# Local and global attention units issued in pairs, with the gate's part moved and the scores further ahead

## The chip, the cores and the metric

The kernel runs on one core of a Trainium2 chip. The core has a matrix engine (TensorE; PE in the profile, with its weight loads shown apart as PEld), a vector engine (VectorE, DVE), a scalar engine for activations (ScalarE, ACT), a general engine (GpSimd, POOL) and a queue engine that issues DMAs (SyncE, SP). Each takes its instructions in the order of the program. The metric is the device time of one execution in microseconds (us), lower is better. A program's time is the median of several runs, and one further execution is recorded by the hardware profiler.

## The reference, cut to what matters

There are 8 batches of 8 heads. Each head has 512 local tokens, 32 global tokens and a width of 64. A local token looks at local tokens within 32 places and at all global tokens; a global token looks at everything.

```python
k_all = np.concatenate([k_g, k_l], axis=2)
s_g = scale * np.matmul(q_g, k_all.transpose(0, 1, 3, 2))
out_g = np.matmul(sm(s_g), v_all)
s_ll = scale * np.matmul(q_l, k_l.transpose(0, 1, 3, 2))
s_ll = np.where(np.abs(pos[:, None] - pos[None, :]) <= 32, s_ll, -1000000000.0)
s_lg = scale * np.matmul(q_l, k_g.transpose(0, 1, 3, 2))
out_l = np.matmul(sm(np.concatenate([s_lg, s_ll], -1)), np.concatenate([v_g, v_l], axis=2))
x = np.concatenate([out_g, out_l], axis=2)
...
logits = x @ w_gate
...
h = np.maximum(x[mask] @ w1[e], 0.0)
out[mask] = h @ w2[e]
```

`sm` is a softmax. The attention rows (4352 rows of 512) go to a mixture of 8 experts: all logits are sorted, each row goes to its best expert that still has room (544 rows each), and each expert is two matrix products with a ReLU between.

## The kernel before

The program has two parts, one after the other: `attention`, which also makes the gate's logits `L`, and `experts`, which starts with a search for the routing over all logits. The change touches `attention` alone.

**Units.** Attention is cut into 80 units, ten for each batch. A `Local` unit takes 256 query rows of one pair of heads (eight per batch); a `Glob` unit takes the global rows of four heads (two per batch). In a batch the order is four Locals, a Glob, four Locals, a Glob; in the last batch two Locals, both Globs, six Locals. Every unit has four steps:

- `a`: the scores, matmuls into PSUM tiles named `S` (L134; of a Glob L195). A Local takes one bank, a Glob two (`sa`, `sb`).
- `e`: on VectorE the mask is added and the row maximum taken (L141), then scaled (L143); on ScalarE four exponentials (L145) write `p`. Of a Glob, the maxima are L201 to L203 and the exponentials L210 to L216, into `pg`, read straight from the two `S` banks.
- `c`: `p` is transposed on TensorE into banks `T` (L150; of a Glob L224, two banks) and copied to SBUF as `pt` or `pgt` by `evac`.
- `d`: the products with the values, into banks `O` (L162; of a Glob L234), then on VectorE the division by the row sums (L165, L166, L170; of a Glob L237 to L241), and DMAs of `xs` or `xg` to DRAM.

PSUM has three banks `S`, three `T` and two `O`. `evac` (L248) shares copies out in the order in which the program makes them: of every five, three go to ScalarE (L251) and two to VectorE (L253).

**The gate's part.** The logits of a batch are made by six small steps (`gate_units`): four times `gate_x` (four transposes of `xs`, L259, and a copy to `xt`), `gate_m` (matmuls with the gate's weights into an `O` bank, L265, and a copy to `ltc`), and `gate_l` (four transposes of `ltc`, L274, and a sum into `L` on VectorE, L275). They stand in a table `extra`, keyed by the number of the iteration: for most batches at 1, 3, 5, 7, 9 and 10 units after the batch's end plus ten; for the batch before the last at six successive units. The global rows of four batches are read back (`load_gx`) and get six steps of the same kind with one block of rows.

**The loop.** It runs over units `i`, with the scores two ahead. TensorE gets, in one iteration, S of unit i+2, T of unit i, O of unit i-1, then the gate's step if there is one. In the program's order `e` of unit i+2 stands between the transposes and the outputs:

```python
units[i + LA].a()
units[i].c()
units[i + LA].e()
units[i - 1].d()
for f in extra.get(i, []): f()
```

Ahead of `a`, SP issues loads of `q`, `qk` and `vw` for the pair of heads four further on; POOL spreads `q` into `qz` (L86). In the last iterations the first steps of the routing (`first`, VectorE, seen as L405) are put in six at a time.

Of the kernel before, what the change touches and what calls it, by code (L numbers as in the profile page):

```python
# [8 lines left out]
F32 = mybir.dt.float32  # L9
# [9 lines left out]
B, H, SL, SG, D = 8, 8, 512, 32, 64  # L19
S = SL + SG  # L20
DM = H * D
# [4 lines left out]
NB = SL // 128  # L26
NW = SL // 32
# [8 lines left out]
def ap_of(t, offset, dims):  # L36
    return bass.AP(tensor=t.tensor, offset=t.offset + offset, ap=dims)
# [27 lines left out]
def attention(ctx, tc, A, consts, xd, ident, L, nbatch, rt=None):  # L65
    nc = tc.nc
    ac = ctx.enter_context(tc.tile_pool(name="ac", bufs=1))
    ld = ctx.enter_context(tc.tile_pool(name="ld", bufs=3))
    wk = ctx.enter_context(tc.tile_pool(name="wk", bufs=3))
# [3 lines left out]
    qk, vw, xs = {}, {}, {}  # L73

    def load_qk(b, p):
        t = ld.tile([128, KW], F32, name="qk", bufs=5)
        q = ld.tile([128, QW], F32, name="q", bufs=3)
        z = qz[(b * NP + p) % NZ]
        nc.sync.dma_start(q, A["qk"][b, p, :, :QW])
        nc.sync.dma_start(t, A["qk"][b, p, :, QW:])  # L80
        qk[b, p] = t

        def spread(eng):
            for h in range(2):
                r = slice(64 * h, 64 * h + 64)
                eng.tensor_copy(z[r, :, h, :], q[r].rearrange("p (j i) -> p j i", i=32))  # L86
        return spread

    def load_v(b, p):
        t = ld.tile([128, 2, NW, D + 1], F32, name="vw", bufs=6)  # L90
        nc.sync.dma_start(t.rearrange("p h w d -> p (h w d)"), A["vw"][b, p])
        vw[b, p] = t

    qz = [ac.tile([128, QW // 32, 2, 32], F32, name=f"qz{i}") for i in range(NZ)]
    pg = [ac.tile([128, 6, 128], F32, name=f"pg{i}") for i in range(2)]
    mask = ac.tile([128, 2 * NB, 128], F32, name="mask")
    wg = ac.tile([128, 4, 32], F32, name="wg")
    P = [(b, p) for b in range(nbatch) for p in range(NP)]
# [6 lines left out]
    for i in range(NZ):  # L105
        nc.gpsimd.memset(qz[i][64:128, :, 0, :], 0.0)
        nc.gpsimd.memset(qz[i][0:64, :, 1, :], 0.0)
    for i in range(2):
        nc.gpsimd.memset(pg[i], 0.0)
    load_qk(0, 0)(nc.vector)  # L110
    nc.sync.dma_start(mask.rearrange("p a b -> p (a b)"), A["mask"])
# [1 line left out]
    spread1 = load_qk(0, 1)  # L113
# [5 lines left out]
    class Local:  # L119
# [3 lines left out]
        def a(s):  # L123
            b, q = s.b, s.q
            z = qz[(b * NP + q) % NZ]
            kw = qk[b, q]
            st = ps.tile([128, NB, 128], F32, name="S", bufs=3)
            s.p = wk.tile([128, NB, 128], F32, name="p", bufs=4)
            s.nm = wk.tile([128, NB], F32, name="nm", bufs=4)
            for c in range(NB):  # L130
                for r in range(2):
                    j = 8 * s.u + 2 * c + r
                    k0 = 32 * ((3 * j + 1) // 2)
                    nc.tensor.matmul(st[64 * r:64 * r + 64, c, :], z[:, j].rearrange("p h i -> p (h i)"),  # L134
                                     kw[:, k0:k0 + 128], start=True, stop=True)
            s.st = st

        def e(s):
            st, nm = s.st, s.nm
            for c in range(NB):  # L140
                nc.vector.tensor_tensor_reduce(s.p[:, c, :], st[:, c, :], mask[:, 4 * s.u + c, :], 1.0, -BIG,  # L141
                                               ALU.add, ALU.max, nm[:, c:c + 1])
            nc.vector.tensor_scalar(nm, nm, -SCALE, None, op0=ALU.mult)  # L143
            for c in range(NB):
                nc.scalar.activation(s.p[:, c, :], s.p[:, c, :], AF.Exp, bias=nm[:, c:c + 1], scale=SCALE)  # L145
# [29 lines left out]
    class Glob:  # L175
# [20 lines left out]

        def e(s):
            b, g = s.b, s.g
            m = wk.tile([128, 8], F32, name="gm", bufs=2)
            s.m = m  # L200
            nc.vector.tensor_reduce(m[:, 0:1], s.sa, axis=AX.X, op=ALU.max)  # L201
            nc.vector.tensor_reduce(m[:, 1:2], s.sb, axis=AX.X, op=ALU.max)
            nc.vector.tensor_scalar(m[:, 2:3], m[:, 0:1], m[:, 1:2], -SCALE, op0=ALU.max, op1=ALU.mult)  # L203
            pgt = pg[(b * 2 + g) % 2]
            s.p = pgt
            f = pgt.rearrange("p a b -> p (a b)")
            d0 = f[:, 0:64]
            d1 = f[:, 512:576]
            pd = list(d0.ap[0])
            nc.scalar.activation(ap_of(d0, 0, [pd, [256, 2], [96, 3], [1, 64]]),  # L210
                                 s.sa[:, 0:384].rearrange("p (a b c) -> p a b c", a=2, c=64), AF.Exp,
                                 bias=m[:, 2:3], scale=SCALE, accum_out=m[:, 3:4])
            nc.scalar.activation(ap_of(d1, 0, [pd, [192, 2], [1, 64]]),
                                 s.sa[:, 384:512].rearrange("p (b c) -> p b c", c=64), AF.Exp,
                                 bias=m[:, 2:3], scale=SCALE, accum_out=m[:, 4:5])
            nc.scalar.activation(f[:, 672:704], s.sb, AF.Exp,  # L216
                                 bias=m[:, 2:3], scale=SCALE, accum_out=m[:, 5:6])
# [30 lines left out]
    def evac(dst, src):  # L248
        nev[0] += 1
        if nev[0] % 5 < 3:  # L250
            nc.scalar.activation(dst, src, AF.Copy)  # L251
        else:
            nc.vector.tensor_copy(dst, src)  # L253

    def gate_x(src, xt, c, spare):
        t = ps.tile([128, NB, 128], F32, name="S" if spare else "T", bufs=3)
        n = src.shape[1]
        for k in range(n):
            nc.tensor.transpose(t[:, k, :], src[:, k, c * 128:(c + 1) * 128], ident)  # L259
        evac(xt[:, c, :n * 128], t[:, :n].rearrange("p a b -> p (a b)"))  # L260

    def gate_m(xt, n):
        lt = ps.tile([128, 512], F32, name="O", bufs=2)
        for c in range(4):
            nc.tensor.matmul(lt[32 * c:32 * c + 32, :n * 128], wg[:, c, :], xt[:, c, :n * 128],  # L265
                             start=True, stop=True)
        ltc = wk.tile([128, 512], F32, name="ltc", bufs=2)
        evac(ltc[:, :n * 128], lt[:, :n * 128])
        return ltc

# [7 lines left out]
    def gate_units(b, src, J, n):  # L278
        xt = []

        def go(c):
            if c == 0:
                xt.append(wk.tile([128, 4, 128 * n], F32, name=f"xt{n}", bufs=2))
            if c < 4:
                gate_x(src(), xt[0], c, b == nbatch - 1)
            elif c == 4:
                xt.append(gate_m(xt[0], n))
            else:
                gate_l(xt[1], J, n)
        return [lambda c=c: go(c) for c in range(6)]  # L290
# [1 line left out]
    gsrc = {}  # L292

    def load_gx(i):
        t = wk.tile([128, 1, DM], F32, name="gx", bufs=2)
        for k in range(4):
            nc.sync.dma_start(t[32 * k:32 * k + 32, 0, :], xd[(4 * i + k) * S:(4 * i + k) * S + SG, :])
        gsrc[i] = t

    units = []  # L300
    for b in range(nbatch):
        loc = [Local(b, h) for h in range(H)]
        gl = [Glob(b, g) for g in range(2)]
        if b < nbatch - 1:
            us = loc[:4] + [gl[0]] + loc[4:] + [gl[1]]
        else:
            us = loc[:2] + gl + loc[2:]
        units += us
    extra = {}
    GS = (0, 2, 4, 6, 8, 9)  # L310
    for b in range(nbatch):
        last = b == nbatch - 1
        s0 = 10 * (b + 1) + 1
        gl = gate_units(b, lambda b=b: gsrc[b // 4], 32 + b // 4, 1) if b % 4 == 3 or last else []
# [13 lines left out]
    nl = [3]  # L328

    def pairidx(u):  # L330
        if isinstance(u, Local):
            return u.b * NP + u.q
        return u.b * NP + 2 * u.g + 1

    nu = len(units)
    first = rt.setup(slice(0, 28)) if rt else None
    LA = 2
    for i in range(-LA, nu + 3):
        if rt and i == 2:
            rt.load()  # L340
        if rt and i == 12:
            rt.prepare()
        if i + LA < nu:
            while nl[0] < len(P) and nl[0] <= pairidx(units[i + LA]) + 4:
                load_qk(*P[nl[0]])(nc.gpsimd)
                load_v(*P[nl[0] - 1])
                nl[0] += 1
                if nl[0] == len(P):
                    load_v(*P[-1])
            units[i + LA].a()  # L350
        if 0 <= i < nu:
            units[i].c()
        if i + LA < nu:
            units[i + LA].e()
            if i + LA == 0:
                spread1(nc.vector)
        if 1 <= i <= nu:
            units[i - 1].d()
        for f in extra.get(i, []):
            f()  # L360
        if rt and i >= nu - 3:
            for _ in range(6):
                next(first, None)


# [638 lines left out]
```

## Time and profile before

| | us |
|---|---|
| timed runs: 752.65, 748.70, 749.91; median | 749.91 |
| the profiled execution's own time | 756.55 |
| its span, first to last instruction | 754.5 |
| attention, up to the first search matmul (L473) | 0 to 236.9 |

The profile's page gives busy times per engine, the span in 40 slices, and groups of instructions by line. The windows view gives the busy times of the engines in a stretch of time. The timeline lists instructions in order of time, with those of one kind merged: start, time from the first start to the last end, engine, line, operation, what it writes and reads, the tile's shape, its count, and in brackets the idle time of the engine before it and what ended that. Matmuls are pipelined, so the rows of two successive groups overlap; what a group takes of TensorE's time is the distance between the starts.

### The profile page before, as it was taken

The page shows a single profiled execution, that of the slowest core. Times are in us where ns is not written, and L with a number is a line of the kernel's source. Part 1 is how long each engine was busy: PE and PEld are TensorE (multiplying, and loading weights), DVE is VectorE, ACT ScalarE, POOL GpSimd, SP SyncE. Part 2 cuts the span into 40 slices and gives each one's busy share as a digit, 9 for nine tenths or more (in the row PEclk, how much of TensorE's full clock was granted, in tenths as well). Part 3 has the DMA queues.
Part 4 walks back from the last instruction along what each step waited for, and adds up shares of the span by engine and source line. Part 5 has one row for each costly group of instructions (what it writes and reads, how often), then busy time and mean ns, then how long its engine had stood idle before and what let it go on. Part 6 is the DMA issues. An engine that isn't in the chain of part 4 may idle for free. (4 is left out here: it accounts for less than half of the span.)

```text
span 754.5 us, 21122 instructions
## 1 busy us (share of the span) xinstructions
PE 697.2 (92%) x8636; PEld 560.2 (74%) x8636; DVE 504.8 (67%) x1848; ACT 313.8 (42%) x849; POOL 159.7 (21%) x190
## 2 busy tenths in 40 slices
PE   7989999999995189999999999999999999899993
PEld 6767777777673179768779878877877878888972
DVE  5887878877777778767767777766776774441300
ACT  3656665665651034234143244234333333443310
POOL 5222112221100130241241241141132043312011
PEclk9999999999998569999999999999999999999997
DMA  9997879969701160360161161261072065231000
GB/s 359 405 364 286 323 280 332 338 244 333 289 22 58 45 238 1 111 204 29 70 234 40 62 240 43 71 212 62 8 260 78 1 254 186 75 126 46 1 33 28
DMA packets 32416, 120.51 MB, mean 160 GB/s; under 512 B 6720, under 2 KB 6976, under 8 KB 24128
## 3 DMA queue, kind: packets, MB, share of 16 engines
q1 hardware_dynamic: 22080, 67.78, 24.1%
q0 software_dynamic: 10240, 51.39, 19.4%
q8 instruction: 68, 1.11, 0.6%
q14 instruction: 28, 0.23, 0.1%
HBM read 101.32 MB, written 17.83 MB: 158 GB/s over the span
## 5 line engine op out<-in xcount | busy, mean ns | idle before, releaser
L860 PE MATMUL H<-xh,w1h 128*128 128x272 f32 x512 | 153.0, 299 | 3.6 <-DVE hl L405 3.0
L860 PE MATMUL H<-xl,w1h 128*128 128x272 f32 x512 | 151.4, 296 | 0.0
L860 PE MATMUL H<-xh,w1l 128*128 128x272 f32 x512 | 151.4, 296 | 0.0
L145 ACT ACTIVATE p<-p,nm 128x128 f32<-128x128 f32 x256 | 82.1, 394 | 65.1 <-DVE ls L165 33.1
L862 ACT ACTIVATE hh<-H 128x272 fp32r<-128x272 f32 x128 | 51.0, 399 | 135.3 <-PE H L860 129.8
L888 PE MATMUL Y<-w2h,hh 128*128 128x512 f32 x256 | 103.9, 406 | 0.0
L860 PEld LDWEIGHTS H<-xh,w1h 128*128 128x128 f32 x512 | 98.0, 191 | 7.0 <-DVE hl L405 2.7
L888 PE MATMUL Y<-w2l,hh 128*128 128x512 f32 x256 | 102.8, 401 | 0.0
L888 PE MATMUL Y<-w2h,hl 128*128 128x512 f32 x256 | 102.4, 400 | 0.0
L860 PEld LDWEIGHTS H<-xl,w1h 128*128 128x128 f32 x512 | 97.9, 191 | 0.6
L860 PEld LDWEIGHTS H<-xh,w1l 128*128 128x128 f32 x512 | 97.8, 191 | 0.3
L134 PE MATMUL S<-qk,qz 128*64 128x128 f32 x1024 | 71.2, 281 | 5.5 <-DVE qz L86 2.9
L405 DVE SCALAR_TENSOR_TENSOR hl<-H,hh 128x272 fp32r<-128x272 f32 x128 | 54.6, 435 | 26.5 <-ACT h L864 12.6
L86 POOL COPY qz<-q 64x544 f32<-64x544 f32 x60 | 38.3, 639 | 149.6 <-DMA q<-in_qk_dram 109.6
L134 PEld LDWEIGHTS S<-qk,qz 128*64 128x64 f32 x1024 | 55.5, 138 | 18.3 <-issue 11.0
L742 POOL DMA_INDIRECT out_dram<-y,idx x40 | 39.7, 992 | 137.9 <-ACT y L833 84.7
L405 DVE TENSOR_TENSOR w2l<-w2r,w2h 128x512 fp32r<-128x512 f32 x64 | 43.2, 688 | 37.6 <-ACT w2h L712 37.2
L696 POOL DMA_INDIRECT w1r<-in_w_dram,widx x16 | 15.7, 979 | 229.8 <-DVE r_a L405 127.2
L141 DVE CUSTOM_DVE_ANT_0 p<-S,mask 128x128 f32<-128x128 f32 x256 | 58.7, 286 | 6.1 <-PE S L134 5.6
L833 ACT ACTIVATE y<-Y 128x512 f32<-128x512 f32 (+1 forms) x40 | 23.2, 595 | 92.8 <-PE Y L888 59.4
L888 PEld LDWEIGHTS Y<-w2h,hh 128*128 128x128 f32 x256 | 48.2, 188 | 15.8 <-issue 5.9
L712 ACT ACTIVATE w1h<-w1r 128x512 fp32r<-128x512 f32 x64 | 36.5, 624 | 49.7 <-DVE L L405 29.8
(168 smaller groups left out, 1200.7 us busy)
## 6 DMA issues: line engine op xcount, KB each, us to landing
vw<-in_vw_dram SPq DMA_DIRECT2D x32, 1040.0 KB, 7.8
qk<-in_qk_dram SPq DMA_DIRECT2D x32, 432.0 KB, 5.4
q<-in_qk_dram SPq DMA_DIRECT2D x32, 272.0 KB, 5.8
xd<-xs SPq DMA_DIRECT2D x8, 1024.0 KB, 6.8
xd<-xg SPq DMA_DIRECT2D x64, 8.0 KB, 5.3
xg<-xd,idx POOLq DMA_INDIRECT x40
out_dram<-y,idx POOLq DMA_INDIRECT x40
mask<-in_mask_dram SPq DMA_DIRECT2D x1, 512.0 KB, 4.5
```

The costliest lines, as they stand in the source:

```text
L86: eng.tensor_copy(z[r, :, h, :], q[r].rearrange("p (j i) -> p j i", i=32))
L134: nc.tensor.matmul(st[64 * r:64 * r + 64, c, :], z[:, j].rearrange("p h i -> p (h i)"), kw[:, k0:k0 + 128], start=True, stop=True)
L141: nc.vector.tensor_tensor_reduce(s.p[:, c, :], st[:, c, :], mask[:, 4 * s.u + c, :], 1.0, -BIG, ALU.add, ALU.max, nm[:, c:c + 1])
L145: nc.scalar.activation(s.p[:, c, :], s.p[:, c, :], AF.Exp, bias=nm[:, c:c + 1], scale=SCALE)
L405: return op(*args, **kw)
L696: nc.gpsimd.indirect_dma_start(out=dst, out_offset=None, in_=src, element_offset=off, in_offset=bass.IndirectOffsetOnAxis(ap=idx, axis=0))
L712: nc.scalar.activation(hi, raw, AF.Copy)
L742: nc.gpsimd.indirect_dma_start(out=out, out_offset=bass.IndirectOffsetOnAxis(ap=rt.idx[ph][:n, t:t + 1], axis=0), in_=y[:n], in_offset=None)
L833: nc.scalar.activation(y[:n], p[:n], AF.Copy)
L860: nc.tensor.matmul(p, w[d][:, fs], x[:, d, q], start=(d + k == 0), stop=(d + k == 5))
L862: nc.scalar.activation(hh[:, f, q], p, AF.Relu)
L888: nc.tensor.matmul(p, h[:, f, q], w[f], start=(f + k == 0), stop=(f + k == 9))
```

## The change

Two units are taken per iteration. The order becomes: transposes of units i and i+1, scores of units i+4 and i+5, the gate's steps of i-1 and i, then `e` of units i+4 and i+5, then the outputs of i and i+1. So the outputs of a unit come in the same iteration as its transposes, and the gate's steps stand between scores and outputs, ahead of `e`. The score, transpose and output banks stay three, three and two. Pools that hold a unit's data for longer get more buffers (`vw` 7, `pg` 3, `p` 6, `nm` 8, `gm` 4), and `ltc`, `xt` and `gx` get one each. In the last batch Locals and Globs alternate at the start. The routing's first steps are put in twelve at a time from unit 76 on.

```diff
-        t = ld.tile([128, 2, NW, D + 1], F32, name="vw", bufs=6)
+        t = ld.tile([128, 2, NW, D + 1], F32, name="vw", bufs=7)
...
-    pg = [ac.tile([128, 6, 128], F32, name=f"pg{i}") for i in range(2)]
+    pg = [ac.tile([128, 6, 128], F32, name=f"pg{i}") for i in range(3)]
...
-            s.p = wk.tile([128, NB, 128], F32, name="p", bufs=4)
-            s.nm = wk.tile([128, NB], F32, name="nm", bufs=4)
+            s.p = wk.tile([128, NB, 128], F32, name="p", bufs=6)
+            s.nm = wk.tile([128, NB], F32, name="nm", bufs=8)
...
-            m = wk.tile([128, 8], F32, name="gm", bufs=2)
+            m = wk.tile([128, 8], F32, name="gm", bufs=4)
...
-            pgt = pg[(b * 2 + g) % 2]
+            pgt = pg[(b * 2 + g) % 3]
...
-        ltc = wk.tile([128, 512], F32, name="ltc", bufs=2)
+        ltc = wk.tile([128, 512], F32, name="ltc", bufs=1)
...
-                xt.append(wk.tile([128, 4, 128 * n], F32, name=f"xt{n}", bufs=2))
+                xt.append(wk.tile([128, 4, 128 * n], F32, name=f"xt{n}", bufs=1))
...
-        t = wk.tile([128, 1, DM], F32, name="gx", bufs=2)
+        t = wk.tile([128, 1, DM], F32, name="gx", bufs=1)
...
-            us = loc[:2] + gl + loc[2:]
+            us = [loc[0], gl[0], loc[1], gl[1]] + loc[2:]
...
-    LA = 2
-    for i in range(-LA, nu + 3):
+    LA = 4
+    for i in range(-4, nu + 2, 2):
+        now = (i, i + 1)
...
-        if i + LA < nu:
-            while nl[0] < len(P) and nl[0] <= pairidx(units[i + LA]) + 4:
-                load_qk(*P[nl[0]])(nc.gpsimd)
-                load_v(*P[nl[0] - 1])
-                nl[0] += 1
-                if nl[0] == len(P):
-                    load_v(*P[-1])
-            units[i + LA].a()
-        if 0 <= i < nu:
-            units[i].c()
-        if i + LA < nu:
-            units[i + LA].e()
-            if i + LA == 0:
-                spread1(nc.vector)
-        if 1 <= i <= nu:
-            units[i - 1].d()
-        for f in extra.get(i, []):
-            f()
-        if rt and i >= nu - 3:
-            for _ in range(6):
+        for k in now:
+            if 0 <= k < nu:
+                units[k].c()
+        for k in now:
+            if k + LA < nu:
+                while nl[0] < len(P) and nl[0] <= pairidx(units[k + LA]) + 4:
+                    load_qk(*P[nl[0]])(nc.gpsimd)
+                    load_v(*P[nl[0] - 1])
+                    nl[0] += 1
+                    if nl[0] == len(P):
+                        load_v(*P[-1])
+                units[k + LA].a()
+        for k in (i - 1, i):
+            for f in extra.get(k, []):
+                f()
+        for k in now:
+            if k + LA < nu:
+                units[k + LA].e()
+                if k + LA == 0:
+                    spread1(nc.vector)
+        for k in now:
+            if 0 <= k < nu:
+                units[k].d()
+        if rt and i >= nu - 4:
+            for _ in range(12):
                 next(first, None)
```

More of the change, by code (lines that the diff above doesn't have):

```diff
@@ L107, in attention @@
         nc.gpsimd.memset(qz[i][0:64, :, 1, :], 0.0)
-    for i in range(2):
+    for i in range(3):
         nc.gpsimd.memset(pg[i], 0.0)
```

## The prediction

> **What bounds the kernel now.** I read the page's busy times and slices first, then the windows of two batches, then TensorE's timeline, group by group.
>
> ```profile
> span 754.5 us, 21122 instructions
> PE 697.2 (92%) x8636; PEld 560.2 (74%) x8636; DVE 504.8 (67%) x1848; ACT 313.8 (42%) x849; POOL 159.7 (21%) x190
> PE   7989999999995189999999999999999999899993
> ```
>
> ```profile
> 10.00:20.00 10.00, 9.93 (x168) 7.43 (x168) 6.73 (x38) 6.23 (x21) 2.55 (x4) 0.83 1.03 412
> 20.00:47.00 27.00, 24.09 (x514) 18.10 (x515) 21.98 (x127) 14.91 (x48) 6.39 (x10) 1.00 1.01 390
> 73.70:100.50 26.80, 26.80 (x571) 20.01 (x570) 21.88 (x120) 16.70 (x54) 5.15 (x9) 1.00 0.83 310
> 100.50:127.70 27.20, 27.15 (x574) 20.20 (x570) 21.53 (x120) 17.96 (x56) 5.08 (x8) 1.00 0.85 308
> ```
>
> A slice is 18.9 us; attention fills the first twelve, up to the dip. The windows (busy us of PE, PEld, DVE, ACT, POOL, then clock, DMA share, GB/s) show one batch of ten units in 26.8 us with PE never idle; DVE has work for 21.9, ACT for 16.7. But a busy PE is a pipelined one, so what a group really costs is the distance from its first start to the next group's:
>
> ```profile
> 113.75 1.09 PE L134 MATMUL S<-qk,qz 128*64 128x128 f32 x16
> 114.77 0.66 PE L150 MATMUL T<-ident,p 128*128 128x128 f32 x4
> 115.36 0.66 PE L162 MATMUL O<-vw,pt 128*32 128x65 f32 x32
> 115.95 1.09 PE L134 MATMUL S<-qk,qz 128*64 128x128 f32 x16
> 116.97 0.88 PE L224 MATMUL T<-ident,pg 128*128 128x128 f32 x6
> 117.78 0.66 PE L162 MATMUL O<-vw,pt 128*32 128x65 f32 x32
> 118.26 1.04 PE L265 MATMUL O<-xt,wg 128*32 128x512 f32 x8
> 119.23 1.09 PE L134 MATMUL S<-qk,qz 128*64 128x128 f32 x16
> ```
>
> Scores S cost 1.02, transposes T 0.59, outputs O 0.59, one after the other with no wait for data: PE's issue order bounds the stage. Part of each cost is not work. Six transposes take 0.81 (116.97 to 117.78) and four 0.59, so one is 0.11 and a group has 0.15 on top. The three kinds use three array shapes (128\*128, 128\*64, 128\*32), and where neighbours have one shape the extra is absent:
>
> ```profile
> 225.45 0.66 PE L259 MATMUL S<-ident,xs 128*128 128x128 f32 x4
> 225.94 0.60 PE L150 MATMUL T<-ident,p 128*128 128x128 f32 x4
> 226.47 0.66 PE L162 MATMUL O<-vw,pt 128*32 128x65 f32 x32
> ```
>
> ```profile
> 5.12 1.97 PE L134 MATMUL S<-qk,qz 128*64 128x128 f32 x32
> ```
>
> Two transposing groups: 1.02 from 225.45 to 226.47, where two apart cost 1.18. Two score groups: 1.97 where one has 1.09, so the second adds 0.88 and not 1.02. And O before the gate's matmul of the same shape takes 0.48 (117.78 to 118.26), not 0.59.
>
> **The change, part by part.** *Pairs.* PE's order becomes T T, S S, gate, O O per two units. Each joint saves 0.15 for T (1.18 less 1.02), 0.14 for S (1.02 less 0.88), 0.13 for O (0.11 at the joint, 0.02 for a first matmul no longer slow). 40 pairs have T and O joints; 39 have a new S joint, the first two score groups being adjacent already. 40 x 0.28 + 39 x 0.14 = **-16.7 us**. The ends are nothing (if the extra belongs to each group's wait) and 17.5; I take 16.7, which the three joints above show.
>
> *Gate transposes* stay groups between S and O, as they were between O and S: 0. Where two now fall in one pair (three times with batch 3's global rows, twice in batch 6) a joint of 0.15 is saved: **-0.75**.
>
> *The gate's matmul* (L265) had O's shape just ahead of it. Now S is ahead, so it pays a switch of 0.11, seven times: **+0.8**.
>
> *Gate matmul and logit transposes in one pair.* Local steps 4 and 5 of batches 0 to 5 fall on units 10(b+1)+9 and +10, which are extras of one iteration, so L274 must wait for the copy of ltc with nothing between. Before, a unit lay between.
>
> ```profile
> 119.37 0.69 DVE L253 COPY ltc<-O 128x512 f32<-128x512 f32 x1
> ```
>
> ```profile
> 235.18 0.60 ACT L251 ACTIVATE ltc<-O 128x512 f32<-128x512 f32 x1 [1.17 <-PE O L265]
> ...
> 235.83 0.65 PE L274 MATMUL T<-ident,ltc 128*128 128x128 f32 x4 [0.49 <-ACT ltc L251]
> ```
>
> The copy starts 1.11 after the matmul (118.26 to 119.37) and lasts 0.69 on DVE or 0.60 on ACT; the transposes follow 0.05 later: 1.76 to 1.85. PE is otherwise free for them 0.97 after (118.26 to 119.23). So it stands idle 0.79 or 0.88. By the program order and the rule of three copies in five to ACT, four of the six go to ACT and two to DVE: 4.9; in batch 6 a transposing group (0.59) of batch 7 lies between, 0.25 left. **+5.1**. It cannot be less; were the copying engine in a Glob's exponentials, up to 1.3 more each, +9.
>
> *The gate's copy ahead of e on its queue.* This is the least certain term. ACT and DVE run their queues in order. Extras now stand before e in the program, so the copy of a gate transpose waits on its engine until PE has passed T T and S S, and the mask steps and exponentials queue behind it.
>
> ```profile
> 115.57 0.28 DVE L141 CUSTOM_DVE_ANT_0 p<-S,mask 128x128 f32<-128x128 f32 x1
> ...
> 116.60 0.15 DVE L165 TENSOR_SCALAR ls<-O 128x4 f32<-128x4 f32 x1
> ...
> 117.35 0.28 DVE L141 CUSTOM_DVE_ANT_0 p<-S,mask 128x128 f32<-128x128 f32 x1
> ```
>
> ```profile
> 107.08 1.29 ACT L145 ACTIVATE p<-p,nm 128x128 f32<-128x128 f32 x4 [2.36 <-DVE nm L143]
> 108.27 0.58 ACT L251 ACTIVATE pt<-T 128x512 f32<-128x512 f32 x1
> ```
>
> On DVE a local unit's e takes 1.03 and its d 0.75; on ACT exponentials take 1.19. A pair of locals with a gate part lasts on PE 1.02 + 1.90 + 0.59 + 1.05 = 4.56. If DVE copies the gate transpose, it starts at 3.7, ends at 4.3, and e e d d end at 7.9: 3.3 into the next pair. That pair's copies of T must be done when O starts, at 3.5: a stall of 0.1 to 0.4. If the next pair holds a Glob, its own transposes fill all three T banks and the gate transpose, due at 3.2 (ten transposes 1.24, S S about 1.95), waits for the first of them to be copied: until 3.95 on DVE, or 3.65 on ACT, whose exponentials end at 3.05. Ten gate transposes before the tail fall on DVE; five are followed by a Glob pair: 3 x 0.45 + 2 x 0.75 = 2.85. Two more delay a Glob's score banks, 0.45 each, and the rest come to about 0.45. **+4.2**, an estimate from these rows; the ends are nothing (the stalls fall where PE waits anyway) and 14 pairs of up to 0.75, +10. Where ACT copies it, it is free again at 2.1 and nothing waits.
>
> *Scores four ahead, larger pools.* PE waited for a bank or code in the start:
>
> ```profile
> 38.36 0.44 PE L234 MATMUL O<-vw,pgt 128*32 128x64 f32 x17 [1.13 <-issue]
> ...
> 45.81 0.66 PE L134 MATMUL S<-qk,qz 128*64 128x128 f32 x8 [1.36 <-issue]
> ...
> 48.98 0.77 PE L134 MATMUL S<-qk,qz 128*64 128x128 f32 x10 [0.75 <-ACT pg L213]
> ```
>
> The last, a score bank held by a Glob, goes: **-0.75**. The "issue" pauses inside groups wait for no data; they fall where the DMA share is 1.01, and I leave them as they are, with 2.5 either way. Loads: the seventh vw buffer lets one load go earlier, the order on SP stays. Scores ask two units (5.4) sooner for their q:
>
> ```profile
> 32.52 1.34 POOL L86 COPY qz<-q 64x544 f32<-64x544 f32 x2 [5.20 <-DMA q<-in_qk_dram]
> ```
>
> This one is ready at 33.9, and the scores that first need it are those around 45.81 above; two units earlier they are at about 39, still later. The third pg memset lengthens POOL's start by 0.7, before it waits for q anyway: 0.
>
> *Tail.* One ltc buffer makes the second logit copy wait for a transpose: **+0.25**. Otherwise the tail is DVE's: the routing's first steps stand in the last pairs,
>
> ```profile
> 226.53 0.37 DVE L405 TENSOR_REDUCE r_m<-L 128x28 f32<-128x224 f32 x1
> ...
> 229.26 0.15 DVE L165 TENSOR_SCALAR ls<-O 128x4 f32<-128x4 f32 x1
> ```
>
> 2.7 us, ahead of the last units' d as before: 0.
>
> Sum: -16.7 - 0.75 + 0.8 + 5.1 + 4.2 - 0.75 + 0.25 = **-7.9 us**. What follows attention starts with the last logits, so all of it moves along: the profiled execution's span would be 746.6 for 754.5. That execution lasted 756.55, the three timed runs have a median of 749.91; taken off that, **742.0**.
>
> [...] At 20 to 47 us PE was idle for 2.9 us in pauses, and the clock stayed at 1.00; at 10 to 20, after PE had stood still, it was 0.83, about 3.4 us at half. [...]
>
> **Rivals.** (a) *The extra per group belongs to the wait with which a group starts, not to the shape.* Then the joints of 16.7 and 0.75 are lost and the costs stay: 749.9 + 9.6 = 759.5, slower. It decides as soon as T T costs 1.18 and not 1.02. Against it: the six transposes at 116.97 go into a second bank in mid-group at an even pace, and 225.94 starts a group of its own without extra. (b) *DVE becomes the bound.* If its queue stalls every pair where it copies a gate part, and Glob copies wait too, +10 to +12 takes the place of +4.2: about 749, no change. For it: DVE has 21.9 of work in a batch that PE would do in 25.6 (26.8, less five pairs of 0.42, and 0.1 and 0.8 for the gate); against it: 3.7 of slack, and scores two pairs ahead. (c) *The queues hide it all*, since scores are early: -12.1, 738. (d) *Half clock* in the seven gate pairs: 3.4 us at half loses 1.7 each, +12: 754.
>
> **How the numbers follow.** Forecast (738 to 746) 0.63; (c), with a little more from the issue pauses, 0.12; (b) 0.15; (a) 0.05; (d) and half-way cases that end slower 0.05. A measurement of this kernel tells about 0.5%, 3.7 us, from no change. Faster than 746.2: forecast and (c), 0.75; within: (b) and a part of (d), 0.17; slower: (a) and the rest, 0.08. The range, 735.0 to 749.5, takes in (c) with quieter code loading and most of (b).
>
> **What would show it.** PE's timeline should have L150 x8 in one row, about 1.02 to the next shape, S x32 about 1.90, O x64 about 1.05. L274 should show an idle time of 0.7 to 0.9 before it, ended by ltc, six times. L259 behind a DVE gate copy should wait for ACT or DVE pt 0.4 to 0.8. A batch should take 25.6 to 26.3 us. I am wrong if the eight transposes keep a gap of 0.15 between them, if O waits for pt in most pairs, or if the clock falls below 1.00 before 230 us.

## The result and the profile after

The changed kernel takes **762.27 us** (median of 4 runs, 759.0 to 766.73), the kernel before 750.41 beside it (4 runs, 748.7 to 752.65). The ratio on record is 1.0133, with a 95% interval of 1.0095 to 1.0170 (the two medians by themselves give 1.016): slower by about 1.3%, where 742.0 was forecast and faster. The execution that was profiled took 762.58, its span is 760.8.

The page of the changed kernel, its span, TensorE's busy time and its slices (19.0 us each):

```profile
span 760.8 us, 21100 instructions
PE 685.0 (90%) x8636; PEld 561.7 (74%) x8636; DVE 503.0 (66%) x1848; ACT 312.0 (41%) x849; POOL 161.1 (21%) x191
PE   7879899799898239999999999999999999999993
```

PE works 12 us less than before (685.0 for 697.2) and the span is 6.3 longer: the saved work is there, and more than that went into standing still. The digits 7 and 8 among the first twelve show where: inside attention, where most slices had been 9. The last logits start at 249.32 us, where they had started at 236.52 (both in DVE's timeline, the last rows of L275). Attention therefore lost 12.8 us; after it the two profiled executions differ by 6.5 the other way, in code that the change doesn't touch.

TensorE's timeline over one pair with a gate matmul and the start of the next:

```profile
96.85 1.09 PE L150 MATMUL T<-ident,p 128*128 128x128 f32 x8
97.88 1.17 PE L195 MATMUL S<-qk,qz 128*64 128x512 f32 x8
98.87 1.07 PE L134 MATMUL S<-qk,qz 128*64 128x128 f32 x16
99.88 1.06 PE L265 MATMUL O<-xt,wg 128*32 128x512 f32 x8
101.78 0.66 PE L274 MATMUL T<-ident,ltc 128*128 128x128 f32 x4 [0.84 <-DVE ltc L253]
102.36 1.11 PE L162 MATMUL O<-vw,pt 128*32 128x65 f32 x64
103.41 1.09 PE L150 MATMUL T<-ident,p 128*128 128x128 f32 x8
104.88 1.97 PE L134 MATMUL S<-qk,qz 128*64 128x128 f32 x32 [0.37 <-ACT pg L213]
106.77 0.66 PE L259 MATMUL T<-ident,xs 128*128 128x128 f32 x4
```

From start to start, O x64 costs 1.05 (102.36 to 103.41), S x32 1.89 (104.88 to 106.77), and T x8 1.03 (96.85 to 97.88): the joints are as forecast. L274 waits 0.84 for ltc, as forecast. In the next pair S waits for a bank that a Global's exponentials hold.

The waits of TensorE between 13 and 228 us (engine, tile, line, what it waited for: us in total, times, longest), first in the kernel before, complete, then in the changed one, complete:

```profile
PE S L134 <- issue: 1.7, 2, 1.4
PE O L234 <- issue: 1.1, 1, 1.1
PE S L134 <- ACT pg L213: 0.7, 1, 0.7
PE O L162 <- issue: 0.4, 1, 0.4
```

```profile
PE O L162 <- issue: 8.2, 5, 3.4
PE O L234 <- issue: 4.6, 5, 1.5
PE T L274 <- ACT ltc L251: 2.9, 4, 0.7
PE S L134 <- ACT pg L213: 2.5, 7, 0.5
PE O L162 <- DVE xs L170: 2.1, 1, 2.1
PE S L134 <- issue: 2.0, 2, 1.8
PE T L274 <- DVE ltc L253: 1.7, 2, 0.8
PE T L150 <- ACT pg L216: 0.9, 1, 0.9
PE T L259 <- ACT pgt L251: 0.6, 1, 0.6
PE T L259 <- ACT pt L251: 0.6, 1, 0.6
```

The largest new item is not data but **"issue": 14.8 us (8.2 + 4.6 + 2.0) in 12 waits, where it had been 3.2 in 4**. Measured from start to start on PE and its weight loads, and without the wait for xs, these are 16 pauses of 20 us for 4 of 4.2. One of them the waits put down to pg L216 (0.9): it stands at such a place too, at 44.5, in the middle of eight transposes that don't read pg. (The expectations below were written with 22 pauses of 23 us, a count that took the wait for xs and a few others in.) Where such a pause stands is regular: counting every matmul, weight load and semaphore instruction of TensorE, the pauses lie 256 instructions apart or a multiple of that, and a packet of 16384 bytes on the instruction queue ends 1.25 to 1.6 us before PE goes on. The longest:

```profile
147.19 0.88 PE L162 MATMUL O<-vw,pt 128*32 128x65 f32 x46
151.50 0.81 PE L162 MATMUL O<-vw,pt 128*32 128x65 f32 x18 [3.44 <-issue]
152.24 1.12 PE L150 MATMUL T<-ident,p 128*128 128x128 f32 x4
153.15 1.49 PE L224 MATMUL T<-ident,pg 128*128 128x128 f32 x6
154.57 2.14 PE L134 MATMUL S<-qk,qz 128*64 128x128 f32 x32
```

The transfers between 148.9 and 150.2 us hold the one code packet of that pause:

```profile
DMA packets 53, 0.05 MB, mean 37 GB/s; under 512 B 39, under 2 KB 39, under 8 KB 52
q8 instruction: 1, 0.02, 5.1%
```

PE stops in the middle of a group of 64, with everything it needs in place. Behind the pause four transposes take 0.91 (152.24 to 153.15) where 0.59 is normal: the clock is low for a while (0.50 from 152 to 154 us), some 1.4 us more, an estimate from the rows from 151.50 on. The window of that batch (busy us of PE, PEld, DVE, ACT, POOL, clock, DMA share, GB/s):

```profile
127.70:154.00 26.30, 19.76 (x418) 15.72 (x417) 16.27 (x91) 13.61 (x44) 3.59 (x6) 0.95 0.85 271
```

Below, 256 instructions of TensorE with the packet that goes with them are called a page of code, and the step from one page to the next a crossing: between 13 and 228 us the trace has 33 crossings and 33 such packets, and the 16 pauses stand at 16 of them.

At the end, DVE's timeline of the changed kernel:

```profile
240.31 0.38 DVE L411 TENSOR_REDUCE r_m<-L 128x28 f32<-128x224 f32 x1
...
242.72 0.39 DVE L411 TENSOR_TENSOR r_oh<-r_v,r_mo 128x224 f16<-128x224 bf16 x1
243.03 0.68 DVE L253 COPY xt<-S 128x512 f32<-128x512 f32 x1
243.63 0.15 DVE L165 TENSOR_SCALAR ls<-O 128x4 f32<-128x4 f32 x1
...
245.11 1.48 DVE L253 COPY xt<-S 128x512 f32<-128x512 f32 x3
```

The last outputs are in PSUM from 241.6, and DVE takes them at 243.6, after the routing's first steps and a gate copy. From the last output matmul to the last logits it is 7.8 us (241.49 to 249.32); before it was 5.35 (231.17 to 236.52).

**The balance.** Joints, forecast and seen: -16.65. Pauses from start to start: +16. Waits for ltc: +4.6. Banks and copies around the gate (2.5 - 0.7 + 0.6 + 0.6; the 0.9 for pg L216 is among the pauses): +3.0. The one wait for xs: +2.1. Half clock: +1.4. Tail: +2.5. Sum +13.0 for a measured 12.8. That it comes out so closely is in part luck, since some waits lie in a slack that another has opened.

### The profile page after: what moved, and what is told of

Read it like the earlier page. It is cut to its first block, busy times and chain, and to the rows that moved or that the text cites. A ratio compares the mean times of both kernels' runs of the same rounds, so it can differ in the third digit from the quotient of the medians.

```text
span 760.8 us, 21100 instructions
## 1 busy us (share of the span) xinstructions
PE 685.0 (90%) x8636; PEld 561.7 (74%) x8636; DVE 503.0 (66%) x1848; ACT 312.0 (41%) x849; POOL 161.1 (21%) x191
## 3 DMA queue, kind: packets, MB, share of 16 engines
q8 instruction: 68, 1.11, 0.6%
## 4 chain that ended last, share of the span: by engine, by line
PE 46%; DVE 4%; issue 2%; ACT 1%; DMA 1%; POOLq 0%; DVEq 0%; ACTq 0%
PE Y L894 21%; PE H L866 18%; PE R L479 3%; PE H L741 2%; PE Y L884 2%; DVE w2l L411 2%; DVE r_G L411 1%; ACT w2h L718 1%; DVE hl L411 0%; DMA xg<-xd,idx 0%; DVE r_pm L411 0%; PE Y L900 0%; DMA out_dram<-y,idx 0%; POOLq L1006 0%; DVE w1l L411 0%
## 5 line engine op out<-in xcount | busy, mean ns | idle before, releaser
L145 ACT ACTIVATE p<-p,nm 128x128 f32<-128x128 f32 x256 | 79.3, 390 | 49.2 <-DVE nm L143 41.1
L134 PE MATMUL S<-qk,qz 128*64 128x128 f32 x1024 | 67.2, 279 | 8.2 <-DVE qz L86 3.5
L411 DVE SCALAR_TENSOR_TENSOR hl<-H,hh 128x272 fp32r<-128x272 f32 x128 | 54.4, 433 | 23.6 <-ACT h L870 12.8
## 6 DMA issues: line engine op xcount, KB each, us to landing
xd<-xs SPq DMA_DIRECT2D x8, 1024.0 KB, 10.2
```

What stands on the lines that cost most here:

```text
L411: return op(*args, **kw)
```

## The experiments

**Theory 1**: TensorE's code pages come late because their packets wait behind the data transfers. **Theory 2**: the paired order uses up pages too fast, whatever the DMA does. **Theory 3**: the gate's waits. Each table gives one run's time beside the kernel before on the same chip, the start of the last logits, the sum of PE's waits put down to "issue" between 13 and 228 us, and the mean time from leaving one code page to the start of the next page's packet (counted in the trace, and good to a few tenths only, since it hangs on which instruction is taken for the crossing). The "issue" sum leaves out a pause that the view puts down to something else. A single profiled execution has pauses of its own: executions of one kernel on one chip differ by up to 9.8 us (the kernel before, 751.16 to 760.96 in 22), so a few us between single executions tell nothing without a wait that explains them.

### Less traffic, smaller pieces

In both kernels value loads were left out:

```diff
     def load_v(b, p):
+        if b * NP + p >= 4:
+            vw[b, p] = vw[0, p]
+            return
```

> The changed kernel with the value loads (vw) of the first four pairs only; all later pairs read those four tiles again, so the output is not the reference's. Theory 1 (TensorE's code pages come late because their packets wait behind the data loads on the DMA): the 22 pauses at page ends (23 us) shrink to under 5 us, a page's packet starts within 1 us of the page before being left (2.98 us now), and the routing's search starts at 228 to 233 us instead of 249.7. Theory 2 (the paired order eats pages in bursts, faster than they can come, whatever else the DMA does): the pauses stay at 18 us or more and the search starts at 245 or later. Theory 3 (the lost time is in the gate's waits): as theory 2, with few pauses gone.

> The same edit in the kernel before (values of the first four pairs only, output not the reference's). Theory 1: its 4.2 us of pauses at page ends go, the search starts at 232 to 234 us instead of 236.9; so the changed kernel without these loads is ahead by 1 to 5 us, where it is behind by 12.8 with them. Theories 2 and 3: no change, 236 to 237, and the changed kernel stays behind by 8 or more.

In both, each value load was cut in four:

```diff
-        nc.sync.dma_start(t.rearrange("p h w d -> p (h w d)"), A["vw"][b, p])
+        f = t.rearrange("p h w d -> p (h w d)")
+        for k in range(4):
+            w = 2 * NW * (D + 1) // 4
+            nc.sync.dma_start(f[:, w * k:w * k + w], A["vw"][b, p][:, w * k:w * k + w])
```

> The changed kernel with each value load issued as four transfers of a quarter of each row (rows of 2080 bytes in place of 8320), the same bytes in all. If a code packet waits for the rows of one transfer that are queued ahead of it on its DMA engine (theory 1a), the wait falls from 2.98 us to about 1, the pauses to 5 to 10 us, and the search starts at 234 to 240. If it waits for whatever is queued, in bytes (theory 1b), or if the pauses are not the DMA's (theory 2), the search starts at 246 to 252, as before the split. Shorter rows could also lower the DMA's rate, and then loads come late: over 252.

> The same split in the kernel before. Theory 1a: pauses from 4.2 us to about 1, the search starts at 233 to 235 instead of 236.9. Theories 1b and 2: 236 to 238.

| run | us | before, same chip | last logits | issue | packet after |
|---|---|---|---|---|---|
| kernel before | 750.41 | | 236.5 | 3.2 | 2.25 |
| changed kernel | 762.27 | 750.41 | 249.3 | 14.8 | 2.98 |
| after_novw | 750.93 | 750.35 | 235.5 | 1.9 | 1.34 |
| before_novw | 749.15 | 750.35 | 235.6 | 1.1 | 1.11 |
| after_vw4 | 752.8 | 750.35 | 238.9 | 7.0 | 2.73 |
| before_vw4 | 748.48 | 750.35 | 235.3 | 1.9 | 2.13 |

Theory 1 holds as far as the loads go: without them the pauses are nearly gone from the changed kernel, and with them 13.8 us of attention, while the kernel before gains 0.9 (last logits at 235.6; the search was expected at 232 to 234). The search, 0.34 after the last logits, starts at 235.8, later than expected (228 to 233): the changed kernel only draws level, so the joints' 16.65 are eaten by the gate and the tail as well, more than I had allowed. Cutting the loads takes away 10.4 us of the changed kernel's attention. But my reason for it (1a) fails: packets still start 2.73 us late, not 1. A delay in step with the bytes of a value row would have gone to a quarter (an estimate, from rows of 2080 bytes for 8320). It went from 2.98 to 2.73 only; how a code packet gets its turn stays open.

### The gate and the tail

These stand on after_vw4, so that pauses hide less. The logit transposes later, then the whole gate part at the end of a pair:

```diff
-    GS = (0, 2, 4, 6, 8, 9)
+    GS = (0, 2, 4, 6, 8, 10)
```

> The changed kernel with the split value loads (as in after_vw4: search at 238.9 us there), and the logit transposes (the last gate step of batches 0 to 5) one pair later than the gate's matmul. If the six waits for ltc (4.8 us of TensorE in that run's waits) stand on the path, they vanish, each with a joint gained or lost of at most 0.15, and the search starts at 233 to 235.5. Rival: the time is given back at the next bank or copy: 237.5 to 239.5.

```diff
-        for k in (i - 1, i):
-            for f in extra.get(k, []):
-                f()
...
         for k in now:
             if 0 <= k < nu:
                 units[k].d()
+        for k in (i - 1, i):
+            for f in extra.get(k, []):
+                f()
```

> The changed kernel with the split value loads, and the gate's part at the end of a pair, behind the mask steps, exponentials and outputs in every engine's queue, not between scores and outputs. Theory Q (a gate copy at the head of ACT's and DVE's queues holds up e and with it copies of T and the score banks): the waits of gate transposes for pt and pgt (2.7 us) and part of the waits of scores for a Global's exponentials (3.3 us) go, about 4 us; besides, gate transposes now stand beside the next pair's T T and the gate's matmul beside O O, so some 28 changes of array shape fall away, 0.15 each, 4 us. The waits for ltc stay (4.8). Search at 229 to 233 instead of 238.9. Rival: the queue costs nothing, and only the shapes count: 234 to 236. Second rival: T's banks bind at the start of each pair, search at 239 or later.

Both edits, with the first three gate steps of the last batch one unit earlier, s0 - (7, 5, 3) for s0 - (6, 4, 2); and the same without the move of the gate part:

> Split value loads, gate part at the end of a pair, logit transposes one pair later, and in the last batch the first three gate steps one unit earlier, so that they run before the last outputs. If all these costs are separate: 238.9 - 4.8 (ltc) - 8 (place) - 2 (tail) = about 224 for the search, total about 738. If they share one cause (TensorE waits elsewhere instead): 229 or later, total 743 or more.

> As a_gs (split value loads, logit transposes one pair later; search at 232.95 us, 7.8 after the last group of outputs), and in the last batch the first three gate steps one unit earlier, so that none of them is left behind the last outputs with the others. If the longer tail of the changed kernel (7.8 us between the last outputs and the last logits, 5.35 before) is that one step and its copy, the tail takes 5.3 to 6.5 and the search starts at 230.5 to 232. Rival: the tail is DVE's (two units' outputs and the routing's first steps at once): 7.5 to 8, search at 233.

The gate's transposes joined to T T where no Global is in the pair (the gate's matmul stays between S and O):

```diff
+        early = not any(0 <= k < nu and isinstance(units[k], Glob) for k in now) and i < nu - 4
+        fs = [f for k in (i - 1, i) for f in extra.get(k, [])]
+        if early:
+            for f in fs:
+                if getattr(f, "t", False):
+                    f()
+            fs = [f for f in fs if not getattr(f, "t", False)]
```

> As a_gstl, with the gate's transposes directly behind the pair's T T where no Global is in the pair (one array shape for twelve transposes), the gate's matmul left between scores and outputs. Some 20 gate steps save a change of shape of 0.15 each, 3 us, and their copies come 1.9 us earlier on ACT's and DVE's queues, so part of the waits for pt and pgt (3.2 us) goes too: search 4 to 6 us ahead of a_gstl's. Rival (pages): faster pairs only run into the next code page sooner, the pauses (10 us) grow, and the gain is under 2. Second rival: T's three banks bind, and the search comes later than in a_gstl.

| run | us | before, same chip | last logits | issue | packet after |
|---|---|---|---|---|---|
| a_gs | 751.65 | 755.94 | 233.0 | 6.4 | 2.74 |
| a_end | 771.72 | 755.94 | 252.4 | 2.3 | 1.85 |
| a_all | 770.63 | 755.94 | 253.3 | 6.9 | 2.55 |
| a_gstl | 757.1 | 757.6 | 239.0 | 7.0 | 2.67 |
| a_tg | 756.54 | 757.6 | 238.5 | 7.6 | 2.53 |

The waits of after_vw4 for ltc, and the only one that is left in a_gs:

```profile
PE T L277 <- ACT ltc L254: 2.9, 4, 0.7
...
PE T L277 <- DVE ltc L256: 1.9, 3, 0.8
```

```profile
PE T L277 <- DVE ltc L256: 0.2, 1, 0.2
```

The ltc wait was on the path: 4.6 of it gone, attention 6.0 shorter in one execution. a_end was a clear miss, 13.5 us later instead of 6 to 10 earlier. Its waits:

```profile
PE T L153 <- ACT xt L254: 7.7, 4, 4.7
PE O L268 <- DVE ls L168: 7.1, 6, 1.5
PE T L227 <- ACT xt L254: 3.1, 3, 1.2
```

Behind the exponentials, the gate's copy reaches ACT late and holds one of the three T banks when the next pair wants them, and the gate's matmul, right after O O, waits for an O bank that DVE hasn't emptied. So the changed kernel's place for the gate, which I charged with 4.2, is far the better one. a_all, with both edits, comes as late (253.3, where about 224 was expected).

a_gstl's tail is 5.5 us as expected, yet the last outputs come 8.3 later than in a_gs: a gate step of batch 7 moved ahead of batch 6's gate matmul, and the two share the one xt buffer. L277 stands 3.55 us for ltc there, and what follows runs slow (O x64 takes 1.89, from 226.76 to 228.65, for 1.05). Its tail proves nothing either, since DVE had time to catch up. a_tg, compared with it, gains 0.5 of the 4 to 6 expected, with 0.6 more in issue waits and DMA busy for 0.95 of 154 to 181 us: that points to the rival, though between two single executions it is not shown.

### Where the late pages come from

More traffic in the kernel before, and the changed kernel with less in pairs (the first unit's outputs put between the two score groups, so that PE's order is T T, S, O, S, gate, O):

```diff
         t = ld.tile([128, 2, NW, D + 1], F32, name="vw", bufs=6)
         nc.sync.dma_start(t.rearrange("p h w d -> p (h w d)"), A["vw"][b, p])
+        nc.sync.dma_start(dump2[:, :], A["vw"][b, p][64:128])
```

> The kernel before with more traffic on the same queue: with each value load a copy of half as many bytes from its input into an unused DRAM tensor (nothing reads it; 32 times 520 KB). Theory 1 (pauses come from code pages that wait behind data): with the DMA busier for longer, pages start 3 us or later on average (2.25 in the kernel before) and pauses grow from 4.2 us to 10 or more, all at page ends, search at 243 or later. Theory 2 (the paired order's bursts are needed for a pause): pauses stay at 3 to 6 us, 236 to 240, unless loads themselves come late, which the waits would show as waits for DMA vw or qk.

```diff
                 units[k + LA].a()
+            if k == i and 0 <= k < nu:
+                units[k].d()
...
-        for k in now:
+        for k in now[1:]:
             if 0 <= k < nu:
                 units[k].d()
```

> The changed kernel with its value loads whole as on record, in the order T T, S, O, S, gate, O: only the transposes stay in pairs. The joints of S and O are lost, 39 x 0.14 + 40 x 0.13 = 10.7 us. If the pauses (23 us) come from bursts, 128 instructions of O O and their weight loads in 1 us, they fall under 10 us and the search starts at 240 to 247. If they come from the mean rate at which pages are used up, which falls by only 0.27 in 3.96 us a pair, they stay at 15 to 20, and the search starts at 252 to 258.

Parts of the change alone: the kernel before with the changed kernel's pools, with LA = 4 and with LA = 2; and the changed kernel with its loads one pair later in program order:

> The kernel before, unit by unit with its own place for the gate, with the changed kernel's pools and scores four units ahead. If the earlier scores and loads alone make the code pages wait (a packet starts 2.25 us after the crossing in the kernel before, 2.98 in the changed one), pauses come to 10 us or more and the search starts at 242 or later. If the pace of the pairs is needed, the pauses stay at 4 to 7 and the search starts at 236 to 239, with at most 3 us from the later first outputs.

> As before_la4 but scores two units ahead, as in the kernel before: only the pools are the changed kernel's (seven vw, six p, three pg, one xt, ltc and gx). If the seventh vw buffer and with it the earlier value loads bring the pauses, search at 243 or later with pauses of 9 or more; if the scores four ahead do, 236 to 238 with pauses of 4 to 7 (before_la4: 249.0, 11.5).

```diff
-                while nl[0] < len(P) and nl[0] <= pairidx(units[k + LA]) + 4:
+                while nl[0] < len(P) and nl[0] <= pairidx(units[k + LA]) + 3:
```

> The changed kernel with loads asked for one pair (two units) later in program order, so that they stand to the outputs as in the kernel before; loads whole. If it is the loads' lead that makes pages late, pauses fall from 23 us to 12 or less and the search comes at 238 to 242 instead of 249.7. If the loads are held by their buffers anyway, nothing moves: 247 to 252. If they come late for the scores, waits for DMA qk or POOL qz show, and the search comes after 252.

| run | us | before, same chip | last logits | issue | packet after |
|---|---|---|---|---|---|
| before_more | 769.79 | 755.94 | 253.4 | 7.7 | 3.34 |
| after_so | 795.03 | 757.6 | 279.2 | 1.0 | 2.28 |
| before_la4 | 766.3 | 757.6 | 249.0 | 10.2 | 2.75 |
| before_pools | 755.34 | 756.55 | 238.0 | 3.8 | 2.32 |
| after_ld3 | 759.44 | 756.55 | 238.6 | 1.8 | 2.25 |

before_more gets pauses without pairs, 7.7 for 3.2; of its 16.9 us in attention they are a part only, since its gate also waits 5.8 for gx and its scores 3.3 for POOL. after_so failed as a test: with one S instead of two ahead of O, pt is not copied yet. Its waits:

```profile
PE O L162 <- ACT pt L251: 12.5, 14, 1.9
PE O L162 <- DVE pt L253: 6.9, 7, 1.7
```

Its pauses vanish, but PE is then so slow that this says nothing about bursts. It shows what S S is for: it covers the copies.

The last three say most. Scores four ahead, *without* pairs, bring issue waits of 10.2 and an attention as late as the whole change (7.0 of its 12.5 us are issue waits more than before; a mean clock of 0.94 from 73.7 to 100.5 is another 1.6, an estimate); the pools alone bring next to nothing (issue 3.8); and the changed kernel with its loads one pair later loses most of the pauses, the issue waits from 14.8 to 1.8, and 10.7 us of attention. PE's "issue" waits of after_ld3, complete (L265 is the gate's matmul), and one wait more:

```profile
PE O L234 <- issue: 0.9, 2, 0.7
PE O L265 <- issue: 0.9, 1, 0.9
```

```profile
PE T L150 <- ACT p L145: 2.3, 1, 2.3
```

The 1.8 flatters it. The wait for p, at 42.9 us, stands at a page's end too, in the middle of a group of transposes, and PE goes on 1.45 us after that page's packet: it is a code pause under another name. Counted from start to start, as the 20 and the 4.2 above, after_ld3 has 4 pauses of 5.3 us: nearly as few as the kernel before.

What that edit moves is SP's order. In the kernel before and in before_pools, the store of a batch's xs stands behind 8, 12, 16, ... value loads (counted in SP's timeline); in the changed kernel and before_la4 behind 9, 13, 17, ...; in after_ld3 behind 8, 12, 16 again. SP's waits between 20 and 208 us, in the changed kernel, then in after_ld3, then in the kernel before, the two largest of each (L79 loads q, L80 qk; L173 stores xs, L243 xg):

```profile
SPq L80 <- PE S L195: 41.8, 10, 8.2
SPq L79 <- DMA xd<-xs: 20.7, 6, 3.7
```

```profile
SPq L243 <- DVE ls L166: 35.3, 5, 9.2
SPq L173 <- DVE gm L238: 34.6, 7, 8.7
```

```profile
SPq L80 <- PE T L150: 48.0, 10, 6.4
SPq L80 <- PE S L195: 17.2, 3, 6.2
```

In the changed kernel, with loads ahead of the stores, SP waits for a free qk buffer and sends loads the moment PE releases one, and the stores queue up behind them; in after_ld3 SP stands 70 us at the stores and the loads wait with it, and the code packet starts 2.25 us after the crossing, as before, and not 2.98. But that can't be the whole of it: the kernel before waits 65 us at qk loads, much as the changed kernel does, and has few pauses. So these runs show that the loads' place matters; how it delays a code packet is not shown.

### All together

The ltc step later, the third gate step of the last batch one unit earlier (6, 4, 3); the value loads cut in four (a_best, a_ld3v) or whole (a_ld3w); in the two a_ld3 runs also the loads one pair later and the copies of the last two iterations on ACT:

```diff
-        if nev[0] % 5 < 3:
+        if nev[0] % 5 < 3 or late[0]:
...
+        late[0] = i >= nu - 2
```

> Split value loads, logit transposes one pair later, and in the last batch only the third gate step one unit earlier (in a_gstl the first one, moved with it, took the one xt buffer while batch 6 still needed it, and ACT stood in that wait). Search at 230 to 232 us instead of a_gs's 232.95, tail 5.3 to 6.5 instead of 7.8. Total 747 to 750 on a chip where the kernel before takes 750.4. Rival: the tail stays at 7.5 (DVE's routing steps), search 233.

> The kernel before with split value loads, timed. Theory 1 gives it 1 to 2 us (pauses 4.6 for 5.3): 748.5 to 750 where the kernel before takes 750.4, within what can be measured; so a_best is 0 to 3 us ahead of it, what is left of the joints' 16.7 after gate waits (7), pauses (5 more) and a later first output (1).

> after_ld3 (loads one pair later in program order, whole; search 238.6, pauses 8.6) with the logit transposes one pair later, the third gate step of the last batch one unit earlier, and all copies of the last two iterations on ACT, which is idle there, not DVE. Each cost by itself: ltc 4.8, DVE's 2 us of copies in the tail: search at 231 to 233.5, last outputs to last logits 5.5 to 7 (8.7 in after_ld3), total 1.0 to 1.8% under the kernel before. Rival: the pauses come back as the pairs get faster (12 us or more): search 236 to 239, total 0 to 0.8% under it.

> The same with the value loads split in four. If the split and the later loads take away the same pauses, nothing is gained over a_ld3w (within 1 us); if they are two different delays of a code page, the pauses fall under 5 us and the search comes 2 to 4 us earlier than in a_ld3w.

| run | median us (n) | before, same chip | ratio, 95% interval | last logits | issue |
|---|---|---|---|---|---|
| a_best | 750.12 (11) | 756.55 | 0.9917, 0.9890 to 0.9944 | 237.3 | 10.1 |
| before_vw4_t | 753.26 (12) | 756.55 | 0.9961, 0.9938 to 0.9984 | 238.4 | 1.2 |
| a_ld3w | 750.19 (7) | 756.15 | 0.9912, 0.9876 to 0.9947 | 231.9 | 2.0 |
| a_ld3v | 748.52 (7) | 756.15 | 0.9901, 0.9871 to 0.9931 | 237.9 | 8.5 |

**Three versions are faster than the kernel before**, by 0.8 to 1.0%; they can't be told from one another. A gain of about the forecast's size was thus to be had, but only with loads and gate step rearranged, and not all of it is the pairs': the split alone gives the kernel before 0.4% (before_vw4_t), a little more than expected. a_best is faster than expected but misses both marks in its profile (last logits at 237.3 for a search at 230 to 232, a tail of 8.8 for 5.3 to 6.5). a_ld3w's 0.9% falls just short of the 1.0 to 1.8% expected, and its profile has the two marks, issue 2.0 and last logits at 231.9. The profile of a_ld3v is its slowest execution (755.53 of 747.03 to 755.53), with issue waits of 8.5 in spite of the later loads: the split does not add to them, and the pauses differ from execution to execution, so the 1.8 and 2.0 rest on two executions against this one. The tail takes 6.5 us in a_ld3w, 8.0 in a_ld3v and 8.8 in a_best: what the copies on ACT are worth is not settled.

## Why the prediction was wrong

- **Pairs, -16.7: right.** All three joints have the size forecast, and rival (a), the extra per group as a wait, is out.
- **Gate transposes joined, -0.75, and the gate's matmul, +0.8**: too small to be told in any run; no row speaks against them.
- **The wait for ltc, +5.1: right.** 2.9 + 1.7 = 4.6 in the waits, six times; a_gs, which removes it, gains 6.0 over after_vw4.
- **The gate's copy ahead of e, +4.2: about right in size** (3.0 in banks and copies, Globals among them), **not in its parts**: gate transposes waited for a copy twice, 1.2 in all, where 2.85 in five pairs was forecast, and the rest is score banks. The other place, a_end, costs 13.5 more. The wait of an output group for xs, 2.1, had no term.
- **A score bank held by a Global, -0.75: wrong in sign.** That wait didn't go; it went from 0.7 once to 2.5 in seven pieces. It is inside the 3.0.
- **"Issue" pauses "left as they are, with 2.5 either way", and loads at 0 because "the order on SP stays": this step failed**, by some 16 us of pauses where 2.5 either way was allowed. The order did not stay: a load is asked for by the unit whose scores come next, so scores two units earlier put each load one pair ahead of the stores. I looked only at when scores need their q. after_ld3 gives the order back, pairs and all: the issue waits fall to 1.8 (5.3 by the stricter count), and attention gets 10.7 of the 20.7 us back by which it missed (12.8 longer, where 7.9 shorter was forecast). Beside the loads the pace may count: the same loads give 10.2 without pairs and 14.8 with them, but between single executions that is not shown.
- **Tail, +0.25: mis-sized**, 2.5. By the timeline above, PE arrives earlier relative to DVE, whose masks, routing steps and copies of two units set the end; no run tests this alone.
- **Half clock (rival d)** came, but behind the longest code pause (0.50 from 152 to 154 us, after 3.44 of waiting) and not in the gate pairs: 1.4 us, the estimate above.
- Rivals (b) and (c): the banks and copies cost 3.0, neither the 10 to 12 of (b) nor the nothing of (c). By time they weren't decided: with most pauses out, after_ld3 is still 0.4% above the kernel before on its chip, in one execution, near (b)'s "no change" without its mechanism.

## What to carry to other kernels

When scores, or any consumer that also asks for loads, move ahead in a program, its loads move too: list each DMA queue's order before and after, stores included, before calling its cost nothing. A row of "issue" waits in the middle of groups, at equal counts of instructions (14.8 us here, 256 instructions apart or a multiple), was here code that arrived late, and a wait at the same count with a data tile's name beside it can be one too. A change of the loads' order, or smaller loads, eased it here without touching the engine (issue waits of 1.8 in after_ld3 and 7.0 in after_vw4), though not in every execution (8.5 in a_ld3v, which has both). Check that what a shorter stage hands over to (here DVE's tail) was not hidden by the time just saved.

## What was not expected of the hardware

A page of 256 TensorE instructions lasts some 5 to 7 us here, up to 9.4 with a pause in it, and its packet took 0.6 to 7.0 us to start in the changed kernel, so it was late at 16 of 33 crossings between 13 and 228 us; each late one cost 0.3 to 3.7 us. PE went on 1.25 to 1.6 us after the packet's end at each of these. With the value loads left out (1040 of 1744 KB a pair) the start fell to 1.1 to 1.3 us on average and the pauses almost vanished; yet at a DMA share of 0.82 to 0.85, about equal in both kernels from 73.7 to 127.7 us, one kernel paused for 3.7 us at five crossings and the other for 0.3 at one. So it is not the share alone; whether it is what is queued at the moment of the crossing was not shown. Ahead of the longest wait, 3.44 us, the late packet stood out 143 to 148.9 us, while the DMA moved 244 GB/s, 192 of 468 packets under 512 bytes, with copies of xg and gx among them; the 37 GB/s above are those of the stretch in which the code packet ran. What makes a code packet late was not settled.
